# Turning the first MLP block's rows by crossbar DMA transposes instead of TensorE

## The chip, the cores and the metric

The kernel runs on one core of a Trainium2 chip. The metric is device time in microseconds (us) of one execution. All times of the kernel before and after come from the same program inputs; the profile is one profiled execution of the same program.

## What is computed

Four layers work on x with 2048 rows (tokens) of 576 values. Layers 1 and 3 are linear attention with 32 heads of 18 values, layers 2 and 4 are an MLP with 4608 hidden values. Each layer adds its result to x.

```python
x = A_x
x = x + _A_ref(_layernorm(x), A_wqkv, A_wo)                  # layer 1
x = x + _B_ref(_layernorm(x), B_w1, B_b1, B_w2, B_b2)        # layer 2
x = x + _A_ref(_layernorm(x), A_wqkv, A_wo)                  # layer 3
x = x + _B_ref(_layernorm(x), B_w1, B_b1, B_w2, B_b2)        # layer 4
# _B_ref(x): y = _layernorm(x); h = gelu(y @ w1 + b1); return h @ w2 + b2
```

## The kernel before, in words

**Tiles and blocks.** The 2048 rows are 16 tiles of 128 rows; four tiles make a block of 512 rows. In the code the layers are li 0 to 3; the text says layers 1 to 4. TensorE contracts over partitions, so the normalized rows are needed turned: `yT` holds five slices of 128 features by 2048 rows (576 features, padded to 640).

**End of an attention layer (`layer_A`, the loop over t).** For each tile t, ten matmuls (L968) multiply the scaled queries `pq` with `kvwo` into a PSUM pair `wo_ps`. There are two such pairs, used in turn (`accA`, `accB`), so tile t+2 takes the pair of tile t. `residual` (L609, VectorE) adds the old x: this is the sum of tile t. It writes the row tile to DRAM (`x_d`, L616, a DMA issued by SyncE). The old x was loaded ahead by `prefetch_xo` (L579 in layer 1, L585 in layer 3), into a pool of nine row buffers (`rows`). A load or a sum that takes a buffer waits until the buffer's former readers and its store are done. Between the tiles, `quarter_stage` (TensorE L842, ScalarE copies L846 into `turned`) and `scale_stage` (L826, L830) broadcast the reciprocal denominators, and VectorE multiplies them into `pq` (L852, L831) for the next block.

**The next MLP's first block.** The sums of tiles 0 to 3 also go into a pipeline, `LNPipe`: statistics (VectorE L391 to L412, or two ScalarE passes L371 and L381), POOL's power and products (L427, L430), the normalized row y written by POOL into one of three buffers `y_ring` (L457, and L467 for the padding), and then the turn. `tick` is called once or twice for each output tile and moves each item one stage on. `hold` counts the ticks that an item waits at first, and `tp_at` is the output tile from which it may be turned. The turn is five TensorE transposes into PSUM (L494, `tp`) and one ScalarE copy to `yT` (L500). The first matmul of the MLP (L1082) reads `yT` of all four tiles.

**The other blocks** are turned in another way: VectorE's 32x32 transposes, then DMAs through DRAM (L295, L305, L320, L323).

**The start-up** of layer 1 turns tiles 8 to 15 by a DMA that transposes (L483), issued by SyncE.

**Order.** The program is written tile by tile, and a scheduler arranges each engine's instructions; each engine and each DMA queue then works in that fixed order. Dependencies with NOSYNC fix an order without a wait. All DMAs of the kernel before are issued by SyncE. Each DMA counts on one of eight semaphores in turn, and waits for the one that used it before.

Of the kernel before, what the change touches and what calls it, by code (L numbers as in the profile page):

```python
# [15 lines left out]
P = 128  # L16
NT = S // P
KD = 5
DPAD = KD * P
# [8 lines left out]
TPC = CB // P  # L28
# [8 lines left out]
def build(tc, A_x, A_wqkv, A_wo, B_w1, B_b1, B_w2, B_b2, out, dbg=None, n_layers=4):  # L37
    nc = tc.nc
    dbg = dbg or {}
    with ExitStack() as ctx:  # L40
# [90 lines left out]
        yT = const.tile([P, KD, S], BF16, name="yT")  # L131
# [137 lines left out]
        state = dict(wo=0, ycnt=0, vcnt=0, turns=0)  # L269
# [69 lines left out]
        class LNPipe:  # L339
            def __init__(self):  # L340
                self.items = []

            def feed(self, xt, t, kind, norm_eng, evac_eng="dve", load_from=None, after=None, hold=0, stats="dve", tp_at=0):
                self.items.append(dict(stage=(0 if load_from is None else -1), xt=xt, t=t, kind=kind,
                                       norm=norm_eng, evac=evac_eng, load=load_from,
                                       after=after, hold=hold, stats=stats, tp_at=tp_at))

            def busy(self):
                return len(self.items)
# [1 line left out]
            def tick(self, transposes=1):  # L351
                land()
                for it in list(self.items):
                    st = it["stage"]
                    if st == 4 and it["evac"] not in ("dma", "xbar"):
                        if transposes == 0 or state["wo"] < it["tp_at"]:
                            continue
                        transposes -= 1
# [3 lines left out]
                    if st == -1:  # L362
                        xn = row_tile("xl")
                        load = nc.sync.dma_start(out=xn[:], in_=x_d[it["load"]])
                        if it["after"] is not None:
                            tc.add_manual_dep(load.ins, it["after"], NOSYNC, reason="loads give way")
                        it["xt"] = xn
                    elif st == 0 and it["stats"] == "act":
                        mv = it["mv"] = work.tile([P, 2], F32, name="ln_mv", bufs=6)
                        it["dump"] = blk.tile([P, D], BF16, name="ln_dump", tag="blk")  # L370
                        one = nc.scalar.activation(out=it["dump"][:], in_=it["xt"][:, 0:D], func=ACT.Identity,  # L371
                                                   scale=-1.0 / D, accum_out=mv[:, 0:1])
                        if it["after"] == "rden":
                            tc.add_manual_dep(one.ins, act_last["copy"], NOSYNC, reason="scalings first")
                        it["stage"] = 0.5
                        if it["kind"] == "B":
                            continue
                    if it["stage"] == 0.5:
                        u = it["u"] = work.tile([P, 1], F32, name="ln_u", bufs=4)
                        mv = it["mv"]  # L380
# [93 lines left out]
                    elif st == 4:  # L474
                        t = it["t"]
                        first_layer = it["kind"] == "A" and it["evac"] in ("act", "xbar")
                        y = it["xt"] if first_layer else it["y"]
                        if it["evac"] == "dma":
                            turn_rows(y, t, it["kind"])
                            self.items.remove(it)  # L480
                            continue
                        if it["evac"] == "xbar":
                            chained(nc.sync.dma_start_transpose(out=yT[:, :, t * P:(t + 1) * P], in_=y[:, 0:DPAD]))  # L483
                            self.items.remove(it)
                            continue
                        tp = ps_h.tile([P, 512], F32, name="tp", tag="h")
                        tp = tp[:, 0:DPAD // 2].bitcast(BF16).rearrange("p (k n) -> p k n", k=KD)
                        first = first_layer and t < 2
                        tp2 = tp
                        if first:  # L490
                            tp2 = ps_h.tile([P, 512], F32, name="tp2", tag="h")
                            tp2 = tp2[:, 0:DPAD // 2].bitcast(BF16).rearrange("p (k n) -> p k n", k=KD)
                        for k in range(KD):
                            pe(nc.tensor.transpose(out=(tp if k < 3 else tp2)[:, k, :], in_=y[:, k * P:(k + 1) * P],  # L494
                                                   identity=ident[:]))
                        if first:
                            named(f"ca{t}", nc.scalar.copy(out=yT[:, 0:3, t * P:(t + 1) * P], in_=tp[:, 0:3, :]))  # L497
                            named(f"cd{t}", nc.vector.tensor_copy(out=yT[:, 3:KD, t * P:(t + 1) * P], in_=tp2[:, 3:KD, :]))
                        elif it["evac"] == "act":
                            turned_tile = nc.scalar.copy(out=yT[:, :, t * P:(t + 1) * P], in_=tp)  # L500
                            act_last["turned"] = turned_tile.ins.name
                            if first_layer and t < 5:
                                named(f"ca{t}", turned_tile)
                            elif act_last["exp"] is not None:
                                tc.add_manual_dep(turned_tile.ins, act_last["exp"], NOSYNC, reason="keys go on first")
                        else:
                            nc.vector.tensor_copy(out=yT[:, :, t * P:(t + 1) * P], in_=tp)
                        self.items.remove(it)
                        continue
# [109 lines left out]
        def layer_A(li, next_kind, pre_a1=None):  # L619
# [352 lines left out]
            def wo_stage(t):  # L972
                wo_products(t, range(wo_open[t][0] if t in wo_open else 0, G))
                wp = wo_open[t][1]
                xn = residual(li, t, wp[:, :, 0:HALF])
                if xn is not None and next_kind == "B" and t < TPC:
                    lnp.feed(xn, t, "B", "pool", "act", hold=(2, 5, 6, 8)[t] if li > 0 else (2, 8, 8, 10)[t], tp_at=6 + 2 * t if li > 0 else (6, 10, 11, 14)[t],
                             **(dict(after="sum") if t in (0, 3 if li > 0 else 2) else dict(stats="act", after="rden")))

            for t in range(AHEAD if li == 0 else AHEAD + 2):  # L980
# [14 lines left out]
            for t in range(NT):  # L995
# [17 lines left out]
                    quad_stage((t + 1) // 2, after=total)  # L1013
                if t == NT - 3:
                    warm_table(ACT.Gelu_apprx_tanh, act_last["copy"])
                if last_pieces and t >= NT - TPC:
                    last_pieces.pop(0)()
                state["wo"] = t
                lnp.tick()
                if t < 10:  # L1020
# [12 lines left out]
        class LayerB:  # L1033
# [70 lines left out]
            def run(self):  # L1104
# [7 lines left out]
                for c in range(NCB):  # L1112
# [2 lines left out]
                        tc.add_manual_dep(zero.ins, act_last["gelu"], NOSYNC, reason="not urgent")  # L1115
                    for g in range(self.done.get(c, 0), NGRP):
                        self.m1_group(c, g)
                        if g in (3, 5):
                            prefetch_xo(li, c * TPC + (g - 3) // 2, add_b2=True)
                        if g in (2, 3, 4, 5):  # L1120
                            feed_next(c, g - 2)
                        lnp.tick(transposes=0)
                        lnp.tick(transposes=0)
# [131 lines left out]
```

## Time and profile before

| | us |
|---|---|
| median of 3 runs | 758.45 (758.22 to 759.66) |
| the profiled execution | 759.16 |
| its span, first to last instruction | 757.2 |
| TensorE busy in it | 750.6 |
| ScalarE / VectorE / POOL busy | 323.3 / 261.3 / 114.9 |

Layer 1 ends and layer 2 starts at 100.14 us of the span; layer 3 ends and layer 4 starts at 472.46. A profile row has start, duration, engine, line, operation and operands; a bracket at its end tells how long the engine was idle before it and what released it. Durations of matmuls contain pipeline time, so their costs are read from start to start.

### The profile page before, as it was taken

The page shows a single profiled execution, that of the slowest core. Times are in us where ns is not written, and L with a number is a line of the kernel's source. Part 1 is how long each engine was busy: PE and PEld are TensorE (multiplying, and loading weights), DVE is VectorE, ACT ScalarE, POOL GpSimd, SP SyncE. Part 2 cuts the span into 40 slices and gives each one's busy share as a digit, 9 for nine tenths or more (in the row PEclk, how much of TensorE's full clock was granted, in tenths as well). Part 3 has the DMA queues.
Part 4 walks back from the last instruction along what each step waited for, and adds up shares of the span by engine and source line. Part 5 has one row for each costly group of instructions (what it writes and reads, how often), then busy time and mean ns, then how long its engine had stood idle before and what let it go on. Part 6 is the DMA issues. An engine that isn't in the chain of part 4 may idle for free.

```text
span 757.2 us, 15677 instructions
## 1 busy us (share of the span) xinstructions
PE 750.6 (99%) x6555; PEld 484.7 (64%) x6555; DVE 261.3 (35%) x641; ACT 323.3 (43%) x722; POOL 114.9 (15%) x219
## 2 busy tenths in 40 slices
PE   8999999999999999999999999999999999999998
PEld 5677754774476457646777777457646754774476
DVE  7766824136034403401366567600230132000000
ACT  5767656105601640373057666660174036205600
POOL 4830313003010201200110004300020020001000
PEclk9999999999999999999999999999999999999999
DMA  8796692226313611411404147430240033011000
GB/s 241 172 246 159 200 350 65 71 65 182 82 40 94 166 51 48 121 54 32 127 24 118 32 137 256 173 83 16 87 106 17 16 126 83 9 32 56 1 9 24
DMA packets 83984, 75.20 MB, mean 99 GB/s; under 512 B 39882, under 2 KB 68554, under 8 KB 83914
## 3 DMA queue, kind: packets, MB, share of 16 engines
q1 hardware_dynamic: 83914, 74.21, 34.5%
q8 instruction: 51, 0.84, 0.5%
q14 instruction: 19, 0.16, 0.1%
HBM read 48.10 MB, written 24.77 MB: 96 GB/s over the span
## 4 chain that ended last, share of the span: by engine, by line
PE 95%; DMA 1%; ACT 1%; DVE 1%; POOL 1%; SPq 0%; issue 0%; POOLq 0%; DVEq 0%
PE m_ps L1144 36%; PE h_ps L1082 21%; PE hp_ps L1082 16%; PE q_ps L625 5%; PE k_ps L657 5%; PE k_ps L699 4%; PE wo_ps L968 3%; PE m_half L1144 1%; DMA xo<-x_d 1%; DMA x<-in_A_x_dram 1%; PE k_tail L699 0%; PE kv_ps L751 0%; ACT turned L846 0%; PE rden_ps L842 0%; PE den_ps L801 0%
## 5 line engine op out<-in xcount | busy, mean ns | idle before, releaser
L1144 PE MATMUL m_ps<-w_sb,hT 128*128 128x288 bf16 x2232 | 274.8, 286 | 0.0
L1144 PEld LDWEIGHTS <-hT 128*128 128x128 bf16 x2304 | 224.2, 98 | 60.4 <-issue 3.4
L1082 PEld LDWEIGHTS <-w_sb 64*128 64x128 bf16 x2304 | 124.5, 94 | 136.4 <-issue 1.9
L1082 PE MATMUL hp_ps<-yT,w_sb 64*128 64x512 bf16 x1152 | 178.0, 376 | 0.0
L1082 PE MATMUL h_ps<-yT,w_sb 64*128 64x512 bf16 x1152 | 148.0, 376 | 0.0
L1087 ACT COPY relay_sb<-relay_sb 128x1 f32<-128x1 f32 x144 | 28.5, 198 | 261.2 <-PE h_ps L1082 218.1
L1078 ACT ACTIVATE hT<-h_ps,b1T 128x512 bf16<-128x512 f32 x144 | 91.1, 683 | 43.8 <-PE h_ps L1082 43.8
L427 POOL TENSOR_TENSOR ln_rstd<-ln_u,neg_half 128x1 f32<-128x1 f32 x61 | 34.3, 563 | 412.3 <-DVE ln_u L409 209.4
L1078 ACT ACTIVATE hT<-hp_ps,b1T 128x512 bf16<-128x512 f32 x144 | 91.1, 692 | 0.0
L609 DVE TENSOR_TENSOR xbf<-m_ps,xo 128x576 bf16<-128x576 f32 x15 | 11.4, 757 | 212.9 <-PE m_ps L1144 212.9
L609 DVE TENSOR_TENSOR xo<-m_ps,xo 128x576 f32<-128x576 f32 x16 | 12.1, 757 | 168.2 <-PE m_ps L1144 168.2
L592 POOL TENSOR_TENSOR xo<-xo,b_bc 128x576 f32<-128x576 f32 x32 | 40.9, 1281 | 115.2 <-DMA xo<-x_d 85.3
L1082 PE MATMUL h_ps<-yT,w_tail 64*128 64x512 bf16 x144 | 54.1, 376 | 0.0
L1082 PE MATMUL hp_ps<-yT,w_tail 64*128 64x512 bf16 x144 | 54.1, 376 | 0.0
L625 PE MATMUL q_ps<-yT,wqkv_sb 128*126 128x512 bf16 (+1 forms) x200 | 49.4, 379 | 0.4 <-DVE pk L546 0.4
L657 PE MATMUL k_ps<-wqkv_sb,yT 128*128 128x288 bf16 x320 | 44.6, 286 | 0.3 <-DMA wqkv_sb<-in_A_wqkv_dram 0.2
L968 PE MATMUL wo_ps<-kvwo,pq 126*128 126x288 bf16 (+1 forms) x320 | 43.5, 286 | 0.6 <-DVE xo L609 0.4
L1082 PEld LDWEIGHTS <-w_tail 64*128 64x128 bf16 x288 | 27.1, 94 | 17.1
L657 PEld LDWEIGHTS <-yT 128*128 128x128 bf16 x320 | 31.0, 98 | 10.6 <-ACT yT L497 0.6
L968 PEld LDWEIGHTS <-pq 126*128 126x128 bf16 (+1 forms) x320 | 30.3, 97 | 9.6 <-issue 1.3
L558 ACT ACTIVATE phi_e<-q_ps 126x512 bf16<-126x512 f32 (+1 forms) x40 | 23.9, 596 | 23.6 <-PE q_ps L625 21.6
L625 PEld LDWEIGHTS <-wqkv_sb 128*126 128x126 bf16 (+1 forms) x200 | 25.7, 131 | 12.3 <-issue 1.0
(151 smaller groups left out, 562.5 us busy)
## 6 DMA issues: line engine op xcount, KB each, us to landing
xo<-x_d SPq DMA_DIRECT2D x48, 288.0 KB
x_d<-xo SPq DMA_DIRECT2D x32, 288.0 KB
xl<-x_d SPq DMA_DIRECT2D x24, 288.0 KB
y_d<-turned SPq DMA_DIRECT2D x40, 144.0 KB
w_sb<-in_B_w_dram SPq DMA_DIRECT2D x6, 864.0 KB
yT<-y_d SPq DMA_DIRECT2D x10, 512.0 KB
w_sb<-in_B_w_dram SPq DMA_DIRECT2D x9, 512.0 KB
x_d<-xn SPq DMA_DIRECT2D x16, 288.0 KB
```

Source lines behind the costliest of these rows:

```text
L427: nc.gpsimd.tensor_tensor(out=rstd[:], in0=it["u"][:], in1=neg_half[:], op=ALU.pow)
L558: exp = nc.scalar.activation(out=e_out, in_=ps_ap, func=ACT.Exp)
L592: nc.gpsimd.tensor_tensor(out=xo[:], in0=xo[:], in1=b2_bc[:], op=ALU.add)
L609: total = nc.vector.tensor_tensor(out=xn[:, cols].rearrange("p (h n) -> p h n", h=2), in0=halves, in1=xo[:, cols].rearrange("p (h n) -> p ...
L625: pe(nc.tensor.matmul(qp[0:GR[g], :], lhsT=wqkv_sb[:, k, GO[g]:GO[g] + GR[g]], rhs=yT[:, k, c * CA:(c + 1) * CA], start=(k == 0), stop=(k ...
L657: pe(nc.tensor.matmul(kp[:, 0:HALF], lhsT=yT[:, k, t * P:(t + 1) * P], rhs=wqkv_sb[:, k, D + half * HALF: D + (half + 1) * HALF], start=(k ...
L699: pe(nc.tensor.matmul(dst, lhsT=lhsT, rhs=pk, start=(t == 0), stop=(t == NT - 1)))
L968: pe(nc.tensor.matmul(wp[:, half, 0:HALF], lhsT=pq[(g, c)][0:GR[g], j * P:(j + 1) * P], rhs=kvwo[g][0:GR[g], half * HALF:(half + 1) * HALF ...
L1078: act_last["gelu"] = nc.scalar.activation(out=to, in_=ps, func=ACT.Gelu_apprx_tanh, bias=b1T[:, f:f + 1], scale=1.0).ins.name
L1082: mm = pe(nc.tensor.matmul(dst[n], lhsT=wt, rhs=mv, start=(seen[n] == 0), stop=(seen[n] == 8)))
L1087: relay = nc.scalar.copy(out=relay_sb[:, 1:2], in_=relay_sb[:, 0:1])
L1144: pe(nc.tensor.matmul(acc[half][:, 0:cols.stop - cols.start], lhsT=hT[f][:, j * P:(j + 1) * P], rhs=w2_sb[:, f, cols], start=(f == 0), sto ...
```

## The change

- For tiles 0 to 3 at the ends of layers 1 and 3, the turn is one `dma_start_transpose` from y to `yT` in place of five transposes and a copy. In layer 1 SyncE issues it, in layer 3 ScalarE, there behind the last of ScalarE's broadcast copies.
- `tp_at` becomes 6, 9, 11, 12 in layer 1 (before: 6, 10, 11, 14) and 5, 8, 10, 12 in layer 3 (before: 6, 8, 10, 12). `hold` in layer 1 becomes 2, 8, 6, 6 (before: 2, 8, 8, 10).
- ScalarE's second pass of statistics (L381) follows the first in the same tick, no longer one tick later.
- The last three loads of w2 (864 KB each) move from tiles 12 to 14 of layer 1 into the first three groups of layer 2.

As a result the scheduler gives VectorE another order in layer 1: the two statistics of tile 2 come ahead of the sum of tile 6 (before: behind it), and the sum of tile 9 comes ahead of all five scalings of block 3 (before: behind three of them). In layer 3 VectorE's order is the same.

```diff
--- before.py
+++ after.py
@@ -340,10 +340,10 @@
             def __init__(self):
                 self.items = []
 
-            def feed(self, xt, t, kind, norm_eng, evac_eng="dve", load_from=None, after=None, hold=0, stats="dve", tp_at=0):
+            def feed(self, xt, t, kind, norm_eng, evac_eng="dve", load_from=None, after=None, hold=0, stats="dve", tp_at=0, queue="sp"):
                 self.items.append(dict(stage=(0 if load_from is None else -1), xt=xt, t=t, kind=kind,
                                        norm=norm_eng, evac=evac_eng, load=load_from,
-                                       after=after, hold=hold, stats=stats, tp_at=tp_at))
+                                       after=after, hold=hold, stats=stats, tp_at=tp_at, queue=queue))
 
             def busy(self):
                 return len(self.items)
@@ -352,6 +352,8 @@
                 land()
                 for it in list(self.items):
                     st = it["stage"]
+                    if st == 4 and it["kind"] == "B" and it["evac"] == "xbar" and state["wo"] < it["tp_at"]:
+                        continue
                     if st == 4 and it["evac"] not in ("dma", "xbar"):
                         if transposes == 0 or state["wo"] < it["tp_at"]:
                             continue
@@ -373,8 +375,6 @@
                         if it["after"] == "rden":
                             tc.add_manual_dep(one.ins, act_last["copy"], NOSYNC, reason="scalings first")
                         it["stage"] = 0.5
-                        if it["kind"] == "B":
-                            continue
                     if it["stage"] == 0.5:
                         u = it["u"] = work.tile([P, 1], F32, name="ln_u", bufs=4)
                         mv = it["mv"]
@@ -479,6 +479,13 @@
                             turn_rows(y, t, it["kind"])
                             self.items.remove(it)
                             continue
+                        if it["evac"] == "xbar" and it["kind"] == "B":
+                            queue = nc.sync if it["queue"] == "sp" else nc.scalar
+                            turn = queue.dma_start_transpose(out=yT[:, :, t * P:(t + 1) * P], in_=y[:, 0:DPAD])
+                            if it["queue"] == "act":
+                                tc.add_manual_dep(turn.ins, act_last["copy"], NOSYNC, reason="scalings first")
+                            self.items.remove(it)
+                            continue
                         if it["evac"] == "xbar":
                             chained(nc.sync.dma_start_transpose(out=yT[:, :, t * P:(t + 1) * P], in_=y[:, 0:DPAD]))
                             self.items.remove(it)
@@ -974,7 +981,8 @@
                 wp = wo_open[t][1]
                 xn = residual(li, t, wp[:, :, 0:HALF])
                 if xn is not None and next_kind == "B" and t < TPC:
-                    lnp.feed(xn, t, "B", "pool", "act", hold=(2, 5, 6, 8)[t] if li > 0 else (2, 8, 8, 10)[t], tp_at=6 + 2 * t if li > 0 else (6, 10, 11, 14)[t],
+                    lnp.feed(xn, t, "B", "pool", "xbar", hold=(2, 5, 6, 8)[t] if li > 0 else (2, 8, 6, 6)[t],
+                             tp_at=(5, 8, 10, 12)[t] if li > 0 else (6, 9, 11, 12)[t], queue="act" if li > 0 else "sp",
                              **(dict(after="sum") if t in (0, 3 if li > 0 else 2) else dict(stats="act", after="rden")))
 
             for t in range(AHEAD if li == 0 else AHEAD + 2):
@@ -1013,8 +1021,6 @@
                     quad_stage((t + 1) // 2, after=total)
                 if t == NT - 3:
                     warm_table(ACT.Gelu_apprx_tanh, act_last["copy"])
-                if last_pieces and t >= NT - TPC:
-                    last_pieces.pop(0)()
                 state["wo"] = t
                 lnp.tick()
                 if t < 10:
@@ -1115,6 +1121,8 @@
                         tc.add_manual_dep(zero.ins, act_last["gelu"], NOSYNC, reason="not urgent")
                     for g in range(self.done.get(c, 0), NGRP):
                         self.m1_group(c, g)
+                        if last_pieces:
+                            last_pieces.pop(0)()
                         if g in (3, 5):
                             prefetch_xo(li, c * TPC + (g - 3) // 2, add_b2=True)
                         if g in (2, 3, 4, 5):
```

## Prediction

> **What bounds the kernel now.** I read the page from the top: busy shares, the clock row, the chain.
>
> ```profile
> span 757.2 us, 15677 instructions
> ...
> PE 750.6 (99%) x6555; PEld 484.7 (64%) x6555; DVE 261.3 (35%) x641; ACT 323.3 (43%) x722; POOL 114.9 (15%) x219
> ...
> PEclk9999999999999999999999999999999999999999
> ...
> PE 95%; DMA 1%; ACT 1%; DVE 1%; POOL 1%; SPq 0%; issue 0%; POOLq 0%; DVEq 0%
> ```
>
> TensorE is busy for 99% of the span at full clock and carries 95% of the chain. So an instruction taken from it shortens the kernel only if nothing else is late at that place. The change acts in two places, the ends of layers 1 and 3, so I read those stretches engine by engine. First TensorE at the end of layer 1 (columns: start, duration, both in us):
>
> ```profile
> 87.11 0.44 PE L494 MATMUL tp<-ident,y_ring 128*128 128x128 bf16 x5
> 87.39 1.40 PE L968 MATMUL wo_ps<-kvwo,pq 126*128 126x288 bf16 x10
> ...
> 94.55 0.44 PE L494 MATMUL tp<-ident,y_ring 128*128 128x128 bf16 x5
> 94.83 3.86 PE L968 MATMUL wo_ps<-kvwo,pq 126*128 126x288 bf16 x30
> 98.53 0.44 PE L494 MATMUL tp<-ident,y_ring 128*128 128x128 bf16 x5
> 98.81 1.40 PE L968 MATMUL wo_ps<-kvwo,pq 126*128 126x288 bf16 x10
> 100.14 1.04 PE L1082 MATMUL h_ps<-yT,w_sb 64*128 64x512 bf16 x8
> ```
>
> Five transposes delay what follows by 0.28 us (87.11 to 87.39); their 0.44 contains pipeline time. An output tile takes 1.23 us (3.70 for the three from 94.83 to 98.53). The MLP starts at 100.14. Now VectorE there:
>
> ```profile
> 88.05 0.75 DVE L609 TENSOR_TENSOR xn<-wo_ps,xo_pair 128x576 f32<-128x576 f32 x1
> 88.72 0.45 DVE L391 BATCH_NORM_STATS2 ln_st<-xn 128x6 f32<-128x288 f32 x1
> 89.08 0.44 DVE L392 BATCH_NORM_STATS2 ln_st<-xn 128x6 f32<-128x288 f32 x1
> ...
> 92.34 0.74 DVE L609 TENSOR_TENSOR xn<-wo_ps,xo_pair 128x576 f32<-128x576 f32 x1
> 93.00 0.74 DVE L852 TENSOR_TENSOR pq<-pq,turned 126x512 bf16<-126x512 bf16 x2
> 93.67 0.74 DVE L609 TENSOR_TENSOR xn<-wo_ps,xo_pair 128x576 f32<-128x576 f32 x1
> ```
>
> These L609 are the residual sums of tiles 6, 9 and 10. VectorE works almost without a gap from 84.63 to 94.4. Output tiles alternate between two PSUM pairs, so tile t+2 can't start before the sum of tile t has ended. VectorE is thus the second limit, a few tenths of a us behind TensorE.
>
> **What is removed.** 40 transposes and their weight loads: eight groups of five, 8 x 0.28 = 2.24 us of TensorE. Eight ScalarE copies (L500, 0.69 each) go too. This is the most the change can gain.
>
> **Layer 1: the VectorE order.** In the changed kernel's order VectorE runs tile 2's two statistics ahead of the sum of tile 6, and the sum of tile 9 ahead of all scalings of block 3. I put the rows' durations into that order:
>
> 1. VectorE is free at 88.05 as before. Two statistics of 0.36 (88.72 to 89.08) come first: sum 6 runs 88.77 to 89.50.
> 2. Tile 8 needs tile 6's bank: it starts at 89.55 (before: 89.10), though TensorE is free earlier.
> 3. Tile 9 follows after 1.24 and a broadcast of 0.22: 91.01. A sum starts 1.44 after its tile: sum 9 at 92.45.
> 4. Only now come sum 9's 0.66, two scalings 0.68, one 0.38, two 0.67: sum 10 runs 94.84 to 95.60 (before: to 94.41).
> 5. Tile 12 needs tile 10's bank: 95.65 (before: 94.83). Three tiles, no transposes: tile 15 at 99.35. With the distance 1.33 of before, the MLP could start at 100.68, **0.54 us later** than now, with all four turns already gone from TensorE.
>
> **Layer 1: the turns on SyncE.** Before has such a DMA in the start-up:
>
> ```profile
> 25.94 1.33 SPq L483 DMA_TRANSPOSE yT<-x  x1
> ```
>
> Issuing takes 1.21 as a median of eight. By the trace's completion records they land 2.74 to 5.05 us after issue starts, median 4.02; the quickest ran with quiet DMA engines. The last turn of layer 1 stands behind the store of tile 11. Sum 11 ends at 96.27 by step 4, the store's issue takes 0.42, and POOL's rows for tile 3 end at about 96.6 (before: 97.16). So it starts at about 96.8 and lands between 99.5 and 101.9, by the median at 100.8. The MLP's first matmul needs all four tiles: I take 0.1 us of waiting, bounds 0 and 1.2. The first turn waits for y of tile 0 (84.39) and holds up the loads of tiles 8 and 9 and the stores of tiles 3 and 4; these land by about 90, and sums 7 and 8 need them at 89.7 and 91.2: at most some tenths, in VectorE's shadow. Layer 1 in sum: **+0.6**, bounds +0.5 and +1.8.
>
> **Layer 3: the turns on ScalarE.** Here VectorE's order stays. Three rows tell what is late:
>
> ```profile
> 463.00 0.78 DVE L852 TENSOR_TENSOR pq<-pq,turned 126x512 bf16<-126x512 bf16 x2 [0.40 <-ACT turned L846]
> ...
> 470.32 0.76 DVE L609 TENSOR_TENSOR xo<-wo_ps,xo 128x576 f32<-128x576 f32 x1 [1.50 <-DMA xo<-x_d]
> ```
>
> ```profile
> 471.14 1.39 PE L968 MATMUL wo_ps<-kvwo,pq 126*128 126x288 bf16 x10 [0.36 <-DVE xo L609]
> ```
>
> ScalarE's copies hold up VectorE at 463.00, which sets sum 9 (464.51 to 465.25) and so tile 11 on TensorE (465.30). In ScalarE's order the first turn replaces the copy at 458.77. No ScalarE issue is in the trace; bounds are nothing and SyncE's 1.33, and I take SyncE's 1.21: 458.40 to 459.61, so L371 (459.36) and all behind it slip by 0.25, tile 11 to 465.55. TensorE, 0.8 us ahead by then, waits that away, and tile 13 starts at 468.13 against 468.15. Three transposes gain nothing and the fourth pays for the slip.
>
> The end of layer 3 is set by the load of tile 13's residual: issued at 464.34, when POOL frees its row, landed at 470.20; sum 13 at 470.32, tile 15 at 471.14. Turns 2 and 3 are issued on ScalarE at about 463.7 and 464.9, into this:
>
> ```profile
> 27.00:28.60 1.60, 1.60 (x11) 0.99 (x10) 1.39 (x5) 0.60 (x2) 1.39 (x3) 1.00 0.57 106
> ...
> 464.00:468.00 4.00, 3.93 (x36) 3.00 (x35) 3.34 (x6) 2.09 (x4) 2.94 (x6) 1.00 1.04 386
> ```
>
> The last two columns are the 16 DMA engines' busy share and GB/s. The upper row holds one turn and almost nothing else: 0.57 x 1.60 = 0.91 us of all engines. The lower row is full. Two turns push the load by up to 1.8 us, less what idles later (share 0.87 from 468 to 471: 0.4 us). Bounds for the start of the MLP: -0.54 (the load comes early enough) and +1.8; I take **+1.2**, nearest to the full row. The last turn (y ready at 467.27) lands by 472.3 by the longest record, before tile 15 is done.
>
> [...]
>
> **Edits at no cost.** The three w2 loads move from tiles 12 to 14 into the MLP's first groups; they landed by 111.3, and the second product starts at 135.21 and needs them some 4 us later, so 28 us cover them. The earlier second statistics pass (a `continue` goes) only advances ScalarE and POOL work off the path.
>
> **Sum.** +0.6 + 1.2 = +1.8. The profiled execution took 759.16 (span 757.2 and 1.96 around it): 760.96. The median, 758.45, is 0.71 lower: **760.25, say 760.3**.
>
> **Rivals.**
> - *Full gain* (chance 0.07): TensorE never waits, 758.45 - 2.24 = 756.2. For it speaks the 99%; against it the two-bank rule. It decides itself at sum 10 of layer 1: that must end by 94.0 instead of 95.6.
> - *Cheap turns* (0.27), not slower: layer 3's load slips by 0.45 or less, with +0.6 in layer 1: between 758.5 and 759.5, say 759.1. For it: turns may fit into the half-idle stretch before 464 (share 0.54 from 461). [...]
> - *Late last turn* (0.16): the turns become what the MLP waits for. If the last one of layer 1 starts when y of before was ready (97.2) and takes the longest record, it lands at 102.25: +2.1; with layer 3's +1.8 this is 762.3.
> - *Forecast* (0.50): 760.3, of itself 759.3 to 761.3.
>
> **Range and chances.** 758.0 to 762.5 leaves out the full gain and the tail of the late turn. A measurement of this kernel tells about 0.2% (1.5 us) from no change, so 756.9 and 760.0 are the limits. Faster 0.08: the full gain and little else. Slower 0.52: the late turn and most of the forecast's case. Same 0.40: the cheap turns and the rest.
>
> **What would show it.** Right: in layer 1 sum 6 behind both statistics, tile 8 near 89.5, tile 12 near 95.6, MLP near 100.7 to 101; in layer 3 tile 13 near 468.1, the load of tile 13 landing after 471, MLP near 473.5. Wrong: tile 12 of layer 1 before 94.8; ScalarE's issue far from 1.2 us; an MLP start that waits for yT by a us or more; a load of tile 13 that lands at 470 or earlier.

## The result and the profile after

| | before | after |
|---|---|---|
| median, six executions of each | 758.56 (758.22 to 759.66) | 765.73 (763.15 to 767.60) |
| ratio of after to before | | 1.0092 (95%: 1.0076 to 1.0108) |
| the profiled execution / its span | 759.16 / 757.2 | 763.15 / 761.3 |
| first MLP matmul of layer 2 / layer 4 | 100.14 / 472.46 | 102.98 / 476.47 |

The change costs 7.2 us (forecast 1.8). A later run of the same kernel gave 763.26 (761.42 to 766.21), ratio 1.0063 (1.0046 to 1.0079). The profile is of the shortest of the first six executions, 2.6 us under their median, and the profiled execution of before was 0.6 above its own. The two profiles so differ by 3.99 us, not 7.2, and the rest is part of the question.

The page of the changed kernel: busy shares and the chain, as shown of before, and the group of the MLP's first matmuls:

```profile
PE 749.7 (98%) x6515; PEld 485.1 (64%) x6515; DVE 260.5 (34%) x641; ACT 318.3 (42%) x714; POOL 114.4 (15%) x219
...
PE 84%; DMA 2%; POOL 1%; DVE 0%; SPq 0%; issue 0%; ACT 0%; POOLq 0%
...
L1088 PE MATMUL h_ps<-yT,w_sb 64*128 64x512 bf16 x1152 | 148.3, 376 | 2.4 <-DMA yT<-y_ring 2.4
```

TensorE has 40 matmuls less and still ends later: the MLP's first matmuls waited 2.4 us for turned rows (before: 0.0). The chain's 84% must not be set beside the 95% of before: the profile follows this chain back only to 87.03 us, and its shares add up to 87%. TensorE at the end of layer 1 (start, duration; in the bracket idle time and what ended it):

```profile
89.47 1.39 PE L975 MATMUL wo_ps<-kvwo,pq 126*128 126x288 bf16 x10 [0.62 <-DVE xn L616]
...
91.95 3.86 PE L975 MATMUL wo_ps<-kvwo,pq 126*128 126x288 bf16 x30 [0.87 <-DVE ln_u L412]
96.52 5.09 PE L975 MATMUL wo_ps<-kvwo,pq 126*128 126x288 bf16 x40 [0.72 <-DVE xn L616]
102.98 1.04 PE L1088 MATMUL h_ps<-yT,w_sb 64*128 64x512 bf16 x8 [1.37 <-DMA yT<-y_ring]
```

These are tiles 8, 9 to 11, 12 to 15, and the MLP. There are four bracketed waits in the place of none, 3.58 us; four turns of 0.28 are gone; the MLP starts 2.84 later. The first comes for the most part from the order of VectorE (0.40 with the order alone, below), and the last is for the last turn. The third is for sum 10: it is 0.32 with the order alone, and the rest follows from the second. The second (0.87) needs VectorE's rows:

```profile
88.68 0.73 DVE L616 TENSOR_TENSOR xn<-wo_ps,xo_pair 128x576 f32<-128x576 f32 x1
...
91.14 0.76 DVE L616 TENSOR_TENSOR xn<-wo_ps,xo_pair 128x576 f32<-128x576 f32 x1 [1.61 <-PE rden_ps L833]
```

Sum 6 (88.68) comes behind two statistics (87.95 and 88.32), as forecast. Sum 7 (91.14) then stands for 1.61 us. The engine named, PE, had been done since 90.9; a wait is put down to the last one of several, and a DMA can be among them. Sum 7 takes the row buffer of tile 4: the trace lists the semaphore of that tile's store among those that sum 7 waits for, and by the completion records the store landed at 91.04. SyncE's queue shows why so late:

```profile
84.33 1.24 SPq L484 DMA_TRANSPOSE yT<-y_ring  x1
85.68 0.51 SPq L586 DMA_DIRECT2D xo_pair<-in_A_x_dram  x1
86.73 1.52 SPq L623 DMA_DIRECT2D x_d<-xn  x2
...
92.56 0.38 SPq L586 DMA_DIRECT2D xo_pair<-in_A_x_dram  x1
93.04 0.46 SPq L623 DMA_DIRECT2D x_d<-xn  x1
93.59 1.35 SPq L484 DMA_TRANSPOSE yT<-y_ring  x1
95.04 0.53 SPq L623 DMA_DIRECT2D x_d<-xn  x1
95.66 0.38 SPq L586 DMA_DIRECT2D xo_pair<-in_A_x_dram  x1
96.09 1.44 SPq L484 DMA_TRANSPOSE yT<-y_ring  x1
97.63 1.01 SPq L623 DMA_DIRECT2D x_d<-xn  x2
98.73 2.15 SPq L484 DMA_TRANSPOSE yT<-y_ring  x1
```

Sum 4 ended at 85.3. Its store, the second of the pair at 86.73, was issued at 87.16, behind the first turn, a load at 85.68 and the store of tile 3. Before, it was the second of this pair, issued at 85.41 and landed at 88.04:

```profile
83.70 2.04 SPq L616 DMA_DIRECT2D x_d<-xn  x2
```

The last turn starts at 98.73 (forecast 96.8) and lands 4.21 us later. From 92.56 on SyncE issues one transfer right behind another, with gaps of at most 0.1 us: the issues of the second and third turn, 1.35 and 1.44 us, are part of the line in which the last one stands. Layer 3, TensorE:

```profile
464.37 6.72 PE L975 MATMUL wo_ps<-kvwo,pq 126*128 126x288 bf16 x50
472.34 1.39 PE L975 MATMUL wo_ps<-kvwo,pq 126*128 126x288 bf16 x10 [1.25 <-DVE xo L616]
...
476.47 1.04 PE L1088 MATMUL h_ps<-yT,w_sb 64*128 64x512 bf16 x8 [1.05 <-DMA yT<-y_ring]
```

Tiles 9 to 13 run through, then tile 14 and (by 0.29, at 474.02) tile 15 wait for sums 12 and 13, these for the residual's loads (landed at 471.41 and 473.02), and the MLP waits for the last turn. From the end of the MLP before it, layer 3 takes 91.75 us (before: 90.59), 1.16 more; 2.84 + 1.16 is the profiled execution's loss.

Which of the waits makes up the 1.16? All times here are 2.84 later because of layer 1, so I take that off and compare with tile 13 of before:

```profile
468.15 2.63 PE L968 MATMUL wo_ps<-kvwo,pq 126*128 126x288 bf16 x20
```

Without the turns TensorE starts tile 13 at 466.85, 1.30 us ahead of before. It waits this lead away at tiles 14 and 15: tile 15 starts at 471.18 (before: 471.14), and the load of tile 13's residual, for which it waits in the end, landed at 470.18 (before: 470.20). The loads cost nothing here against before. What is lost is lost behind tile 15, to the last turn. A second profile of the same kernel says the same: counted from the start of layer 3, tile 15 starts 0.06 us earlier than before, and the MLP waits 1.65 us.

### The profile page after: what moved, and what is told of

The parts are those of the page before. It is cut to its first block, busy times and chain, and to the rows that moved or that the text cites. A ratio compares the mean times of both kernels' runs of the same rounds, so it can differ in the third digit from the quotient of the medians.

```text
span 761.3 us, 15613 instructions
## 1 busy us (share of the span) xinstructions
PE 749.7 (98%) x6515; PEld 485.1 (64%) x6515; DVE 260.5 (34%) x641; ACT 318.3 (42%) x714; POOL 114.4 (15%) x219
## 4 chain that ended last, share of the span: by engine, by line
PE 84%; DMA 2%; POOL 1%; DVE 0%; SPq 0%; issue 0%; ACT 0%; POOLq 0%
PE m_ps L1152 36%; PE h_ps L1088 20%; PE hp_ps L1088 16%; PE q_ps L632 3%; PE k_ps L664 3%; PE k_ps L706 2%; DMA yT<-y_ring 1%; PE wo_ps L975 1%; PE m_half L1152 1%; DMA x_d<-xn 0%; POOL y_ring L457 0%; DMA xo_pair<-in_A_x_dram 0%; PE k_tail L706 0%; POOL ln_nmr L430 0%; PE rden_ps L849 0%
## 5 line engine op out<-in xcount | busy, mean ns | idle before, releaser
L1088 PEld LDWEIGHTS <-w_sb 64*128 64x128 bf16 x2304 | 126.6, 94 | 136.7 <-issue 2.8
L599 POOL TENSOR_TENSOR xo<-xo,b_bc 128x576 f32<-128x576 f32 x32 | 40.9, 1284 | 117.2 <-DMA xo<-x_d 96.8
```

The lines of the kernel that those rows point to most:

```text
L599: nc.gpsimd.tensor_tensor(out=xo[:], in0=xo[:], in1=b2_bc[:], op=ALU.add)
L1088: mm = pe(nc.tensor.matmul(dst[n], lhsT=wt, rhs=mv, start=(seen[n] == 0), stop=(seen[n] == 8)))
```

## The experiments

All medians stand beside 758.4 to 758.6 for before, measured in the same session. Layer 1 has a start-up whose length varies by up to 2.4 us between the profiled executions, so I compare its end from tile 5's start to the MLP: before 15.49, after 18.43.

### One layer at a time, the order alone, another queue

Layer 1 alone (the other run is the mirror image):

```diff
-lnp.feed(xn, t, "B", "pool", "xbar", ...
+lnp.feed(xn, t, "B", "pool", "act" if li > 0 else "xbar", ...   # hold, tp_at and the continue of before for "act"
```

> DMA turns in layer 1 alone (issued by SyncE as in the changed kernel), layer 3 as before the change. Theory A (in layer 1 the first turn stands on SyncE's queue ahead of the store of tile 4, whose row buffer sum 7 waits for, and the last turn lands 4.2 us after it was issued): layer 1 keeps its whole loss, the first MLP matmul of layer 2 at about 103.0 us against 100.1 before, and layer 3 loses nothing: 2.84 us over the kernel before in a profiled execution, so 761.4 us by the median of before. Rival B (what is lost is lost to the transfers as such, alike for each of the eight turns): half of the changed kernel's loss, 7.2 / 2 = 3.6 us, 762.1 us. The 2.6 us by which the median of the changed kernel is above its profiled execution is explained by neither: where it belongs to layer 1, this run's median is near 764 and its runs are spread by 4 us as those of the changed kernel are.

> DMA turns in layer 3 alone (issued by ScalarE as in the changed kernel), layer 1's turns and order as before. Theory A: layer 3 loses its own 1.17 us (the loads of the residual of tiles 12 and 13 land late, sum 12 and sum 13 wait for them, and the last turn lands after tile 15 is done): 759.7 us. Rival B (each turn costs the same): 3.6 us, 762.1 us. Where the spread of the changed kernel's runs belongs to layer 3, the median here is near 762 and the runs are spread by 4 us; where it belongs to layer 1, they stay within 1.5 us.

Layer 1 alone: **761.90** (760.83 to 762.68), ratio 1.0040 (1.0028 to 1.0053). Layer 3 alone: **765.80** (764.28 to 767.12), 1.0093 (1.0080 to 1.0105). Layer 1 lies between its two theories (761.4 and 762.1) and by its median separates neither; by its profile it keeps 2.35 of the 2.94 us from tile 5 to the MLP (17.84). Layer 3 decides against rival B: alone it costs as much as both together, and neither theory had that. The profile of layer 3 alone shows sums 12 and 13 and the MLP waiting again, but longer (1.55, 1.90 and 2.81 on TensorE), turns 3 and 4 landing 10.7 us after their issue (in the changed kernel 7.6 and 6.6), and, new, an MLP of layer 4 of 283.77 us, where before and after both had 281.90. Here the load of tile 13's residual does land late, 2.3 us later after the start of the layer than before.

All steps of the change, but the turns by TensorE:

```diff
-lnp.feed(xn, t, "B", "pool", "xbar", ...
+lnp.feed(xn, t, "B", "pool", "act", ...
```

> All of the changed kernel's moved steps (holds, output tiles of the turns, the second half of the statistics at once, w2 loads later), but the turns made by TensorE as before. Theory A (the DMA turns are what makes sum 7 and the MLP of layers 2 and 4 late): sum 7 does not wait for the store of tile 4, tile 9 does not stall for 0.87 us, and the MLP of layer 2 starts within 0.9 us of before (0.5 us for the tiles 12 that come later): 758.6 to 759.5 us. Rival C (the order of VectorE alone, statistics ahead of sums): tile 9 and tile 12 stall as in the changed kernel, 0.87 and 0.72 us, and the time is 760 us or more.

**759.19** (758.38 to 760.47), 1.0009 (1.0001 to 1.0018). TensorE waits 0.40 at tile 8 and 0.32 at tile 12 and not at tile 9; tile 5 to the MLP takes 16.42. Theory A holds: the order is worth 0.9 us of layer 1, and the rest comes with the transfers.

```diff
-queue="act" if li > 0 else "sp",
+queue="act",
```

> The changed kernel with layer 1's four turns issued by ScalarE in place of SyncE. Theory A (head of line on SyncE: the first turn's issue of 1.24 us stands ahead of a load and of the store of tile 4): the store of tile 4 is issued about 1.2 us earlier, sum 7's wait of 1.61 us falls to about 0.4 us, tile 9 starts about 0.9 us earlier, and what is left of layer 1's loss is the last turn: 764.3 us by the median where it lands 4.2 us after its issue, as on SyncE, 766 to 767 where it lands 6 to 7.6 us after, as ScalarE's turns of layer 3 did. Rival B (the transfers of the turn hold up the store's landing, whoever issues it): the store still lands at about 91.0 us, sum 7 still waits 1.6 us, and the time is that of the changed kernel or more.

**769.43** (767.54 to 772.02), more than either landing time had given. TensorE at the end of layer 1:

```profile
90.74 3.86 PE L975 MATMUL wo_ps<-kvwo,pq 126*128 126x288 bf16 x30
...
105.61 1.89 PE L1088 MATMUL h_ps<-yT,w_sb 64*128 64x512 bf16 x8 [5.20 <-DMA yT<-y_ring]
```

Tile 9 no longer waits (90.74, against 91.95). The store of tile 4 was issued at 85.14 and landed at 87.93, and sum 7 started at 89.28 without idling: the store behind SyncE's turn was what held it up. The landing of that store and the start of sum 7 were 91.04 and 91.14 in the changed kernel, 89.34 and 89.44 with the order alone. But the last turn now lands 9.6 us after its issue: SyncE, no longer in line with it, sends a w2 load of 864 KB ahead of it (95.31), and TensorE idles for 5.20 us. That this load is the reason is not shown by a run of its own; before, the four stores right behind the w2 load of 95.25 also landed 7.5 to 8.0 us after their issue. That matmul row also lasts 1.89, not 1.04: TensorE runs at half clock (0.50 granted from 105.61 to 109.61).

### Queue, crossbar or pieces

```diff
-queue="act" if li > 0 else "sp",
+queue="sp",
```

> The changed kernel with layer 3's four turns issued by SyncE too, in line with the residual's loads and the stores, in place of ScalarE. What the first four runs showed: the turns of layer 3 alone cost 7.3 us and their landing takes up to 10.7 us; those of layer 1 alone cost 3.5 us; after a long stall the granted clock is 0.50 for some microseconds. Theory A (two queues that share the 16 DMA engines hold each other up, in one queue a turn lands about 4 us after it is issued): landing of layer 3's turns 2.7 to 5 us, the MLP of layer 4 waits less than 2.5 us for the last, the clock stays 1.00, and the median is 762.5 to 764 us with runs within 2 us of each other. Rival B (it is the transfer, whoever issues it): landing up to 7 to 10 us again, 765.7 us or more, with clocks of 0.995 to 0.998.

**768.14** (767.30 to 768.94). The landing part was right, the time wrong. The turns land 2.6 to 5.2 us after their issue, and no tile waits:

```profile
463.48 9.46 PE L975 MATMUL wo_ps<-kvwo,pq 126*128 126x288 bf16 x70
479.03 1.46 PE L1088 MATMUL h_ps<-yT,w_sb 64*128 64x512 bf16 x6 [6.09 <-issue]
```

All seven tiles 9 to 15 run in one piece. But in SyncE's fixed order the turns stand behind stores of tiles that are not summed yet: turn 3 is issued at 471.75, two stores from 473.89, the last turn at 474.98, and TensorE stands for 6.09 us. On ScalarE a turn is issued in time and lands late (the last two of the changed kernel after 7.6 and 6.6 us); on SyncE it lands in time (2.6 to 5.2) and is issued late (474.98).

```diff
-turn = queue.dma_start_transpose(out=yT[:, :, t * P:(t + 1) * P], in_=y[:, 0:DPAD])
+turn = queue.dma_start(out=yT[:, :, t * P:(t + 1) * P], in_=y[:, 0:DPAD].rearrange("p (k n) -> p k n", k=KD))
```

This edit was made for layer 3, for both layers, and (in the next part) with layer 3 alone.

> The changed kernel with layer 3's four turns replaced by plain copies on ScalarE's queue, of the same bytes between the same buffers in the same 256-byte pieces; the rows are not turned, so the second MLP block computes with wrong operands. Theory A (the second queue with its small pieces beside SyncE's transfers): landing 5 to 10 us again and the time of the changed kernel, 764 to 766 us. Rival C (the crossbar itself is what holds the other transfers up): landing 2 to 4 us, the loads of the residual land within 4 us as before the change, layer 3 loses under 0.5 us, and the median is 761.5 to 762.5 us, that of layer 1 alone.

> Plain copies of the same bytes in the same 256-byte pieces in place of all eight turns, on the same queues as in the changed kernel (layer 1 SyncE, layer 3 ScalarE); no rows are turned, so both first MLP blocks compute with wrong operands. With copies in layer 3 alone the time was 761.8 us, and layer 1's turns by crossbar alone 761.9. Theory A (the crossbar is what costs, in layer 1 too): copies land in 2 to 3 us, the last ahead of tile 15's end or within 0.5 us of it; what is left of layer 1 is the order of VectorE and the store of tile 4 behind the first copy (0.75 to 1.5 us), and the median is 759.2 to 760.5 us. Rival B (in layer 1 it is SyncE's order and the late issue of the last turn, whatever the kind of transfer): 761.5 to 762.5 us.

In layer 3: **761.83** (760.49 to 763.71), 1.0042 (1.0029 to 1.0055): by the time it is rival C, the crossbar. Its other half failed: the last three copies landed 5.6 to 6.3 us after their issue, not 2 to 4, and the profiled execution still lost 0.9 us in layer 3. In both: **761.62** (760.61 to 762.31), 1.0033 (1.0020 to 1.0046): rival B, so in layer 1 it does not matter whether SyncE's transfer turns or copies. VectorE of that kernel in layer 1 now names the DMA itself:

```profile
91.88 0.76 DVE L616 TENSOR_TENSOR xn<-wo_ps,xo_pair 128x576 f32<-128x576 f32 x1 [2.68 <-DMA x_d<-xn]
```

It is sum 7 behind the store of tile 4 (landed at 91.78) again, with a copy ahead of it on SyncE.

### The crossbar measured on one chip

> Layer 3 alone as in the run with its four turns by ScalarE (765.8 us), but with plain copies of the same bytes in the same 256-byte pieces; the order on every engine is the same to the instruction. The rows are not turned, so the MLP of layer 4 computes with wrong operands. Theory A (it is the crossbar: while a turn is in flight the other transfers of the core stand for 1 to 2.4 us, so the residual's loads and the next turn are late): copies land within 6.5 us, ordinary 2304-byte packets take about 100 ns on the mean and not 176, and the median is 759 to 760.5 us, 5 us and more under the next run. Rival B (the second queue with its small pieces, or the late issue): 764 us or more, like the next run.

> The kernel with layer 3's four turns by ScalarE once more, beside the run with copies on the same chip: 764.5 to 767 us if what it lost is its own (five executions gave 764.3 to 767.1), about 762.5 us if the first time was that chip's, as the changed kernel's two medians, 765.7 and 763.3 us, differ.

Copies: **761.12** (759.71 to 766.81), 1.0050 (1.0029 to 1.0071). Turns: **765.22** (761.51 to 766.29), 1.0082 (1.0067 to 1.0098). The programs differ in the kind of transfer alone, and their medians by 4.1 us. The executions overlap, and so, barely, do the intervals; by the ratios the difference is 2.4 us. That turns cost more than copies fits the five earlier executions of the same kernel with turns (764.28 to 767.12); how much more is known only as 2 to 4 us. The 2.7 us that the copies cost were more than theory A had, and their last two landed 6.8 and 8.1 us after issue, not within 6.5: a part of the loss is not the crossbar's. The DMA queues in the same 14 us (461 to 475), copies first (a queue's packets, MB, share of the 16 engines' time):

```profile
DMA packets 3972, 4.62 MB, mean 330 GB/s; under 512 B 2190, under 2 KB 2190, under 8 KB 3970
...
q1 hardware_dynamic: 2002, 4.10, 80.0%
q10 hardware_dynamic: 1968, 0.49, 15.7%
```

and turns:

```profile
DMA packets 2997, 2.70 MB, mean 193 GB/s; under 512 B 2038, under 2 KB 2038, under 8 KB 2996
...
q1 hardware_dynamic: 1072, 2.21, 71.2%
q10 hardware_dynamic: 1924, 0.48, 30.6%
```

q1 is SyncE's queue, q10 ScalarE's. The turns' own packets take twice the time of the copies' (30.6% against 15.7%), and SyncE's loads and stores move 2.21 MB in 71.2% of the time where they moved 4.10 MB in 80.0%: 1.6 times the time for a byte. (This is the better measure than GB/s, since SyncE does not issue the same transfers in this stretch of the two runs.) The 16 engines look as busy as before and move 193 GB/s in place of 330. Between 455 and 478 us the 2304-byte packets took 136 ns on the mean beside turns, 102 ns beside copies, and 107 ns before the change; in all three the median is 93 ns, so it is a few packets that stand long.

In layer 3 the long packets came only with both, the crossbar and the second queue. Where SyncE issued the turns of layer 3 in line with its own transfers, the 2304-byte packets took 99 ns on the mean while a turn was in flight, as beside copies; where ScalarE issued them, 168 and 147 ns with layer 3 alone and 125 ns in the changed kernel. In layer 1 they took 106 ns beside SyncE's turns. With layer 1's turns on ScalarE it was 103 ns, so both together do not always bring them; what else layer 3 has is open.

### The clock

The windows of the run with turns, cut where the granted clock changes (length, TensorE busy, instructions, PEclk, DMA share, GB/s):

```profile
468.35:471.76 3.41, 1.43 (x11) 1.00 1.26 213
471.76:475.17 3.41, 2.56 (x10) 0.50 1.08 154
...
478.59:482.00 3.41, 3.41 (x18) 0.50 1.03 400
482.00:485.41 3.41, 3.41 (x34) 1.00 1.04 390
```

After a period in which TensorE was busy for 1.43 of 3.41 us, it gets half clock for 10.24 us. The MLP starts in it (476.92), runs 5.1 us at half speed and takes 284.39 us in place of 281.90. Here the clock comes back after one full period (478.59 to 482.00); at half clock, the periods with 75 and 49% did not bring it back. In the run with 6 and 6 fillers below, a period with TensorE busy throughout (476.44 to 479.86) did not either, only the next one. In all the traces the changes stand 3.41 us or a multiple of it apart (10.24 us here, 6.83 in that run). Of the periods at full clock on that grid, the kernel's end left out, nine with TensorE busy for 46% or less were followed by half clock, one with 44% (in a start-up) was not, and none with 47% or more was. So 46% busy did not keep the full clock here.

Keeping TensorE at work in the wait, with 20 and 16 such matmuls (fillers) in the kernel with layer 1's turns by ScalarE, with 6 and 6 in the changed kernel:

```diff
+for _ in range({1: 20, 3: 16}.get(self.li, 0) if c == 0 and g == 0 else 0):      # the other run: {1: 6, 3: 6}
+    pe(nc.tensor.matmul(dst[0], lhsT=w1_sb[0:64, 0, 0:P], rhs=w1_sb[0:64, 1, 0:512], start=True, stop=True))
```

> The kernel with layer 1's turns on ScalarE (769.4 us), and in the waits for the last turn TensorE is kept at work by 20 (layer 1) and 16 (layer 3) matmuls of 64 rows by 512 columns into a bank that the MLP then starts anew. Theory A (the granted clock falls to 0.50 because TensorE stood idle for 4 us): the clock stays 1.00, the two stretches at half clock, 2.97 and 1.65 us of lost work in the profiled execution, are gone, and the median is 764.5 to 766 us. Rival B (the clock falls for another reason, such as the DMA load, which these matmuls do not change): 769 us or, with the fillers' own time, more.

> The changed kernel itself, beside the next one on the same chip. The first profile of it was of its fastest execution (763.15 us, clock 1.00 throughout, TensorE waits of 1.37 and 1.05 us for the two last turns); the others took up to 767.6 us. Theory A (in the slower ones the last turn or the residual's loads land later, TensorE is busy for less than about half of one 3.4 us period and runs the next one or two at half clock): median 765 to 766.5 us again, the slow executions with mean clocks of 0.996 to 0.998, and a profile of one shows a stretch of 3.4 or 6.8 us at 0.50 around the start of one of the two MLPs, whose end comes 1.5 to 2 us later for it. Rival B (the spread has nothing to do with the clock): a profile of a slow execution with clock 1.00 and the time lost elsewhere.

> The changed kernel with 6 matmuls of 64 rows by 512 columns (0.224 us each in the run with 20 and 16 of them, 1.34 us in all) between tile 15 and the MLP of layers 2 and 4. Theory A (the half clock makes up most of the 2.6 us between the fastest execution and the median): median 763.3 to 764.5 us, clocks of 0.998 and more, runs within 2.5 us. Rival B (the later landing itself makes it up, and the clock little): median 765 to 766.5 us, as without the fillers, with the clocks nearer to 1.00.

With 20 and 16 fillers: **772.05** (767.63 to 776.71). In the profiled execution the clock stayed at 1.00 and both MLPs took 281.9 us; it took 767.63, 4.4 less than the profiled one without fillers (772.02; 2.97 + 1.65 = 4.6 forecast). But this sets the fastest of six executions with fillers beside the slowest of four without. The other five had mean clocks of 0.991 to 0.998, and the median did not fall, it rose by 2.6: that expectation failed. That idleness lowers the clock rests on the nine periods; the one profile with fillers agrees with it. The changed kernel again: **763.26** (761.42 to 766.21), under the 765 to 766.5 that was expected. With 6 and 6 fillers: **767.59** (763.83 to 769.96), 4.3 above it, a failure too. Its profile shows the fillers in the wrong place for this:

```profile
475.52 1.71 PE L975 MATMUL wo_ps<-kvwo,pq 126*128 126x288 bf16 x10 [2.74 <-DVE xo L616]
477.16 2.74 PE L1069 MATMUL h_ps<-w_sb 64*128 64x512 bf16 x6
480.05 1.89 PE L1091 MATMUL h_ps<-yT,w_sb 64*128 64x512 bf16 x8 [0.15 <-DMA yT<-y_ring]
```

The stand of 2.74 us ahead of the last tile, for a residual's load, had already lowered the clock (half from 476.44 to 483.27); the fillers themselves ran in it. Turns 3 and 4 of that execution landed 9.6 and 10.9 us after issue. Why these kernels' turns land later on the whole than the changed kernel's is not settled.

The changed kernel's twelve executions, by mean granted clock: six at 0.999 to 1.000 took 761.4 to 764.0 us, three at 0.998 763.4 to 766.6, three at 0.996 766.2 to 767.6. No profile of the changed kernel itself caught a lowered clock ahead of an MLP. That its spread is this mechanism is argued from these clocks and from the profiles of the other kernels, not shown.

### Where a turn by DMA costs nothing

```diff
+first_turn = dict(evac_eng="xbar", queue="act") if t == 0 else dict(evac_eng="act")    # layer 3 only: if t == 0 and li > 0; two turns: if t < 2 and li > 0
```

> Only the first of the four turns of each layer by DMA, issued by ScalarE at output tile 6, the other three by TensorE at the tiles and with the order of before; the loads of w2 later as in the changed kernel. Theory A (the harm is in the last turns, which nothing covers, and in the transfers that run beside the later ones): the two TensorE turns saved are all that is left, 2 times 0.28 us: 757.9 us, within 0.2% of before. Rival B (any turn by DMA delays a store or a load on which an output tile waits): 759.5 us or more.

> The kernel before with one turn moved: the first of layer 3 by DMA, issued by ScalarE at output tile 6, when the 16 DMA engines stand idle. In the profile with the first turns of both layers, layer 3 took 1.19 us less than before (0.28 us of TensorE, tile 14's wait of 0.36 us gone) and layer 1 took 0.42 us more. Theory A (a turn by DMA pays where nothing else is in flight and its landing has 10 us to spare): 757.5 to 758.2 us, 0.3 to 0.9 us under before. Rival B (the gain was that execution's own): within 0.2 us of before, 758.3 to 758.7 us.

> The kernel before with the first two turns of layer 3 by DMA on ScalarE's queue (output tiles 6 and 8), the last two by TensorE. The first alone gave 758.0 us. Theory A (the harm sets in where a turn meets the residual's loads and stores): the second turn, issued as they start, lands 5 to 7 us after its issue and holds a load up; 0.28 us of TensorE is saved and tiles 11 to 13 wait up to 1.5 us: 758.3 to 760 us. Rival B (only the last turn, which nothing covers, does harm): 757.4 to 757.8 us.

First turns of both layers: **759.20** (758.03 to 761.21), 1.0010 (1.0002 to 1.0019): between the two theories; in layer 1 tile 5 to the MLP takes 16.20 us, 0.71 more than before. First turn of layer 3 alone: **758.01** (757.62 to 761.53), 0.9998 (0.9987 to 1.0008): the median is in theory A's range, but no difference is shown. Both profiles agree on layer 3, 89.40 and 89.42 us (before: 90.59); this turn lands in 3.5 us, with the engines idle. Two turns: **760.71** (759.62 to 765.01), 1.0028 (1.0016 to 1.0040), a little over theory A's range. The second turn meets the loads, lands after 6.5 us, and tiles wait 0.86 and 1.45 us for sums (in the profile, of the slowest execution). In layer 3 harm begins with the second turn, not with the last. No version tried is shown to beat the kernel before.

## Why the prediction was wrong

The direction was right, the size (1.8 against 7.2 us) far off and the time outside the range. What failed in the changed kernel: the store of tile 4 was put in VectorE's shadow, the wait for the last turn was put at 0.1 us in layer 1 and at nothing in layer 3, and the load in layer 3, put at 1.2, cost nothing. The clock was taken as given. Point by point:

- **What is removed** (2.24 us): never seen as a gain at an MLP's start, except for the one turn of layer 3 that ran alone.
- **VectorE's order in layer 1, steps 1 and 2**: right. Sum 6 at 88.68 (forecast 88.77), tile 8 at 89.47 (89.55). The order alone costs 0.9 us in layer 1 by the trace, and 0.8 for both layers by the median; forecast 0.54.
- **Step 3 (tile 9 at 91.01) failed, by "at most some tenths, in VectorE's shadow"**. Tile 9 started at 91.95. I saw that the stores of tiles 3 and 4 stand behind the first turn, and put their landing at "about 90". It was 91.04: issued 1.9 us after the sum's end, landed 3.9 us after that. Sum 7 needs the buffer, VectorE stood for 1.61 us and TensorE for 0.87. Taking the turn off SyncE removed that wait.
- **The last turn of layer 1**: the term "I take 0.1 us of waiting, bounds 0 and 1.2" was mis-sized. The latency (4.21) was in its bounds (2.74 to 5.05), but the turn started at 98.73, not at 96.8. I reckoned one store's issue ahead of it, from the end of sum 11; in fact SyncE issued without a pause from 92.56 on, the two turns before it among the rest. Wait: 1.37. Layer 1 in all 2.84, forecast 0.6.
- **ScalarE's slip in layer 3**: wrong. Issues took 1.22 to 2.02 and delayed no tile: tiles 9 to 13 ran through, and TensorE was 1.30 us ahead at tile 13, where I had it level.
- **The load of the residual** (+1.2, bound 1.8): failed in the changed kernel. Sums 12 and 13 wait for loads, but the load of tile 13 landed at 470.18 on the scale of before, no later than before, and tile 15 lost 0.04 us. With layer 3 alone the mechanism did act: tile 15 starts 2.3 and 1.7 us later after the start of the layer. There the price, 0.91 us of the engines for a turn that ran alone, was too low: a byte of the others took 1.6 times as long.
- **"The last turn lands by 472.3, before tile 15 is done"**: failed. It landed at 476.33, 473.5 on the scale of before, and the MLP waited 1.05. That layer 3 came out at 1.16 in the profiled execution, as forecast, is luck: the load, put at 1.2, cost nothing, and the last turn, put at nothing, cost all of it. Alone layer 3 cost 7.4 and 6.8 us.
- **The clock**: missing. I read PEclk of before, all nines, as given. Stalls of 1.8 us and more in one period of 3.41 brought half clock (after nine of ten such periods), and 5.1 us at half clock cost the MLP 2.49 us (284.39 against 281.90); by that I estimate up to 1.7 us for a period.
- **The rivals**: "late last turn" named the right kind of wait, and the sign against the forecast, an MLP that waits for yT by a us or more, came true in both layers. Its 2.1 for layer 1 was too much for that wait (1.37) and less than the whole (2.84); for layer 3 it took the load's bound; and it was given 0.16. "Cheap turns" let the load of layer 3 slip by 0.45 us at most, and no run shows the 0.45: in the changed kernel that load slipped by nothing (470.18 against 470.20), with layer 3 alone by 2.3 us. Nor were turns cheap there: the same program took 765.22 us with turns and 761.12 with copies. w2's loads in their new place delayed nothing that was seen; ahead of the last turn one may have been a loss (the run by ScalarE).

**What stays open.** Of the 7.2 us between the medians the two profiles explain 3.99; the rest is put down to later landing and half clock, by argument. Layers 1 and 3 alone cost 3.5 and about 7 us, both together 4.7 and 7.2: not a sum. In the changed kernel layer 3's turns landed in 4.8 to 7.6 us, alone in up to 10.7, with the same order on every engine of the layer. Nor is it known why one kernel's turns land sooner in one execution than in another.

## What to carry to other kernels

An instruction taken from a full engine is a gain only if the wait that comes in its place is shorter (here 0.28 us a turn against a wait of 1.37). A transfer that replaces it must be issued in time and land in time, and on a DMA queue with a fixed order it must not stand ahead of a store whose buffer is wanted back (the store of tile 4 landed at 91.04, before at 88.04). Price a transfer by one that ran beside the same traffic, not by one that ran alone (a byte of the others took 1.6 times as long beside turns). Where TensorE may be busy for 46% or less of 3.41 us, as in the nine periods that half clock followed, add the cost of half clock to the stall (2.49 us for 5.1 us of the MLP).

## What the runs showed of the hardware

- In layer 3, with turns on ScalarE's queue beside SyncE's transfers, the core moved 193 GB/s, against 330 with plain copies of the same bytes in the same stretch, and a byte of SyncE's transfers took 1.6 times as long. With the turns on SyncE's own queue its packets were not slowed (99 ns on the mean, 102 beside copies).
- A turn landed 2.6 to 3.6 us after issue with the engines idle or lightly loaded (share 0.39 from 84.3 to 87.0 of the changed kernel), 3.0 to 5.2 us in line on a loaded SyncE, and mostly 5 to 11 us on ScalarE's queue beside SyncE's; plain copies there took 5.2 to 8.1 us too, once loads ran. The two queues' shares of the 16 engines, 71.2% and 30.6%, add up to about 100% from 461 to 475 us of the run with turns.
- To issue a transposing DMA held a queue for 1.2 to 2.4 us on SyncE or ScalarE, a plain copy of the same bytes mostly for 0.6 to 0.7.
- Half clock for TensorE followed nine of ten periods of 3.41 us with 46% or less of it busy, and lasted 3.4 to 10.2 us.
